# A delta-rule recurrence with an MoE layer on one Trainium2 core: recurrence products on four 64x64 quarters of the array

## The chip, the cores and the metric

The kernel runs on one core of one Trainium2 chip. The metric is device time in microseconds (us), the median of several executions. The core has a TensorE (matrix products, PE in the profile, with its weight loads as PEld), a VectorE (DVE), a ScalarE (ACT), a GpSimd (POOL) and a SyncE (SP), whose queue issues nearly all transfers here. Each engine works through its own list of instructions in order and waits on semaphores for the others.

## The reference

Two parts follow each other. The first is a recurrence over 768 time steps for 4 batches x 8 heads with head size 48:

```
k_n = k / (norm(k) + 1e-06)
for t in range(S):
    y[t]  = q[t] @ state
    v_old = state^T @ k_n[t]
    state = state + beta[t] * outer(k_n[t], v[t] - v_old)
```

The second is an MoE-shaped layer on the 3072 tokens, whose 384 features are all heads' y side by side: `h = x @ w_in` (384 x 2048), an activation `g` that is 0 below -1, h above 1 and (h+1)^2/4 between, and `g @ w_out` (2048 x 384). Everything is fp32.

## The kernel before

The sequence is cut into 12 blocks of 64 steps; block g is worked out for all 32 (batch, head) pairs at once. Two blocks make a group G (0 to 5). Within a block the recurrence is solved in closed form: the Gram matrix of the keys (64x64 for each pair), a triangular solve on it, and four small products by pair, which hang together from block to block through the state SU:

- r (`chain_r`, L338): keys times state, which VectorE subtracts from the values KV (L343);
- u (`chain_u`, L352): the solved triangle XT times r, which ScalarE copies into SU (L356);
- y (`chain_y`, L372): queries times state and masked query Gram times u, the block's output, split by ScalarE and VectorE (L377 to L382) into a rounded part and its rest, for the MoE layer; a fourth of it is moved between partitions by six transfers (xb, L386);
- d (`chain_d`, L396): keys times u, which VectorE adds to the state (L407).

A pair occupies 64 rows of the array: of each two heads one has its keys on rows 0 to 47, the other on rows 64 to 111. A product of r, then, has its stationary operand on one half of the rows and its result on one half of the columns, and the two heads of such a couple lie on opposite halves of both. In u the result stays on the rows' own side. The 32 pairs are 16 such couples (NU), in two halves i of eight (NT, NV); each half has its own tile W (keys, queries, and the masked query Gram that is written back into it), its own KV, its own PSUM bank and its own evictions. `gram` (L146, L147) makes a keys' Gram and a keys-with-queries Gram by one product of 128 moving columns, four couples to a bank.

`lanes`, `solve`, `unlanes` (and their `_whole` forms from group 2 on) solve the triangles of a group's two blocks, largely on VectorE, from the transposition L204 to the transposition into XT (L257, L270); `merge16` and `merge32` finish them with tiny products on 32x32 tiles.

The order is written out by hand. Before the main loop the first group runs alone, with L473 (20 products of 512 columns on idle data) on TensorE while VectorE solves. Weights arrive packed; a generator `unpack` (L125 to L137) unpacks one after the other between other work. In the main loop an item is an up product (L524, 9 instructions), the activation, and a down product two items later (L539). The tables `pe` and `fill` say which small product stands behind which up or down product: `pe` at a whole step comes between up and down, at a half step behind down. `products` issues TensorE's part of all pieces at a step, and `finish` then issues their evictions, those of a half step at the next item's start. In group 0 the items are half as wide at both ends. In a step the last d of a group and the first two Grams of the next stand together. Recurrence products take their PSUM from the two banks `ch`; in the start `spare` hands out all eight.

Loads are issued by SP in the order of the program: xb transfers of a block, W and KV of the block two further on, the stores of finished output.

## Time and profile before

| what | value |
|---|---|
| time, median of 3 runs | 694.93 us (694.51 to 697.15) |
| the profiled execution, first to last instruction (its span) | 693.4 us |
| PE busy | 637.4 us (92%) |
| DVE busy | 437.2 us (63%) |
| ACT busy | 397.7 us (57%) |
| DMA | 41.45 MB, mean 60 GB/s |
| granted clock of TensorE, mean | 0.956 |

The profiled execution has no device time of its own besides the span; the runs' median lies 1.5 us above it. In the page a busy time is the union of an engine's instructions; matmuls are pipelined, so their ends are modelled and a mean duration of one (some 220 ns for a recurrence product) is longer than the pace at which they follow each other. The pace is read from the chain of waits or the timeline: a stage's length divided by its records. An fp32 product leaves two records for each matmul of the program. In the chain of waits each line is the work, or the wait, that the end depended on, with start and length in us.

### The profile page before, as it was taken

How to read it: one execution, taken by the hardware profiler on the slowest of the kernel's cores; microseconds unless marked ns; L12 is line 12 of the kernel's file. 1: busy time of each engine (PE TensorE's matmuls, PEld its weight loads, DVE VectorE, ACT ScalarE, POOL GpSimd, SP SyncE). 2: the span in 40 equal slices, each digit the busy share in tenths (PEclk: the TensorE clock that was granted, in tenths of full speed). 3: DMA queues.
4: the chain of work that ended last, by engine and by line, in shares of the span. 5: the costliest groups of instructions: out<-in, count | busy, mean ns of one | idle time of the engine just before them, and what ended most of it. 6: DMA issues, size and time to landing. Idle time of an engine off the chain costs nothing.

```text
span 693.4 us, 19365 instructions
## 1 busy us (share of the span) xinstructions
PE 637.4 (92%) x8428; PEld 552.6 (80%) x8428; DVE 437.2 (63%) x920; ACT 397.7 (57%) x720; POOL 44.8 (6%) x90
## 2 busy tenths in 40 slices
PE   9848876899999899999999999999999999999996
PEld 7338765678989788888888888788888788889895
DVE  3848788973455896446896447895457894433332
ACT  4227785556656556644457545557555468556663
POOL 3203042001000200000200000200000200000000
PEclk9956896799999999999999999999999999999999
DMA  8960430000161000043100153100242000001001
GB/s 244 418 267 9 120 103 1 0 3 4 24 171 53 24 1 2 18 109 98 46 2 2 41 122 81 28 1 2 60 123 79 9 1 3 14 12 46 0 1 46
DMA packets 18532, 41.45 MB, mean 60 GB/s; under 512 B 3600, under 2 KB 9104, under 8 KB 18448
## 3 DMA queue, kind: packets, MB, share of 16 engines
q1 hardware_dynamic: 18112, 40.04, 20.0%
q8 instruction: 66, 1.08, 0.7%
q14 instruction: 18, 0.15, 0.1%
q0 software_dynamic: 256, 0.08, 0.1%
q10 hardware_dynamic: 80, 0.10, 0.1%
HBM read 33.13 MB, written 4.72 MB: 55 GB/s over the span
## 4 chain that ended last, share of the span: by engine, by line
PE 54%; DVE 29%; ACT 6%; issue 5%; DMA 2%; SPq 2%; POOL 1%; DVEq 0%; POOLq 0%; ACTq 0%
PE o L539 17%; PE h L524 16%; DVE pr L247 5%; DVE A L249 4%; PE ch L146 4%; DVE glo L643 4%; PE ch L372 3%; DVE s L674 3%; PE ch L352 3%; PE ch L324 2%; PE ch L396 2%; DVE A L204 2%; PE ch L308 2%; DMA W<-in_kqa_dram 2%; PE ch L338 2%
## 5 line engine op out<-in xcount | busy, mean ns | idle before, releaser
L524 PE MATMUL h<-xb,wt 128*128 128x512 f32 (+1 forms) x936 | 230.6, 392 | 11.9 <-DVE s L674 10.6
L524 PEld LDWEIGHTS h<-xb,wt 128*128 128x128 f32 x936 | 166.5, 193 | 50.1 <-DVE s L674 15.8
L539 PE MATMUL o<-wt,ghi 128*128 128x384 f32 x768 | 201.7, 344 | 0.0
L539 PEld LDWEIGHTS o<-wt,ghi 128*128 128x128 f32 x768 | 138.9, 190 | 8.6 <-issue 1.5
L674 DVE TENSOR_TENSOR s<-h,s 128x512 f32<-128x512 f32 (+1 forms) x104 | 67.0, 644 | 112.9 <-ACT s L666 112.5
L539 PE MATMUL o<-wt,glo 128*128 128x384 f32 x384 | 130.9, 341 | 5.8 <-DVE glo L643 5.8
L642 ACT CAST ghi<-s 128x512 fp32r<-128x512 f32 (+1 forms) x104 | 61.3, 589 | 110.4 <-DVE s L674 81.4
L647 ACT ACTIVATE s<-h,half 128x512 f32<-128x512 f32 (+1 forms) x104 | 68.0, 654 | 55.8 <-PE h L524 55.1
L643 DVE TENSOR_TENSOR glo<-s,ghi 128x512 fp32r<-128x512 f32 (+1 forms) x104 | 67.1, 645 | 36.3 <-ACT ghi L642 35.9
L539 PEld LDWEIGHTS o<-wt,glo 128*128 128x128 f32 x384 | 72.8, 190 | 8.0 <-DVE glo L643 8.0
L647 ACT ACTIVATE s<-s,one 128x512 f32<-128x512 f32 (+1 forms) x104 | 71.8, 691 | 2.6
L666 ACT ACTIVATE s<-s 128x512 f32<-128x512 f32 (+1 forms) x104 | 62.3, 599 | 3.3
L146 PE MATMUL ch<-W 48*64 48x128 f32 x336 | 43.1, 278 | 9.3 <-ACT W L155 3.7
L146 PEld LDWEIGHTS ch<-W 48*64 48x64 f32 x336 | 37.2, 136 | 14.9 <-issue 5.5
L147 PE MATMUL ch<-W 48*64 48x128 f32 x336 | 43.4, 279 | 0.0
L247 DVE TENSOR_TENSOR pr<-A 128x30 f32<-128x30 f32 (+14 forms) x120 | 39.4, 328 | 5.5 <-POOL A L218 3.3
L249 DVE TENSOR_TENSOR A<-A,pr 128x30 f32<-128x30 f32 (+14 forms) x120 | 39.8, 332 | 4.4
L163 DVE TENSOR_TENSOR W<-ch,mask 64x256 f32<-64x256 f32 x64 | 27.0, 422 | 18.9 <-ACT GG L150 18.1
L150 ACT COPY GG<-ch 128x256 f32<-128x256 f32 x42 | 15.4, 374 | 38.5 <-PE ch L147 38.5
L147 PEld LDWEIGHTS ch<-W 48*64 48x64 f32 x336 | 37.2, 136 | 0.0
L218 POOL TENSOR_SCALAR_AFFINE_SELECT A<-A 128x1024 f32<-128x1024 f32 x4 | 5.1, 1265 | 365.4 <-DVE A L217 365.4
L407 DVE TENSOR_TENSOR SU<-ch,SU 48x384 f32<-48x384 f32 x40 | 22.2, 555 | 9.2 <-PE ch L396 8.5
(137 smaller groups left out, 705.6 us busy)
## 6 DMA issues: line engine op xcount, KB each, us to landing
wt<-in_w_dram SPq DMA_DIRECT2D x16, 768.0 KB, 13.7
KV<-in_kv_dram SPq DMA_DIRECT2D x24, 384.0 KB, 5.7
W<-in_kqb_dram SPq DMA_DIRECT2D x24, 256.0 KB, 4.7
W<-in_kqa_dram SPq DMA_DIRECT2D x24, 192.0 KB, 4.8
out_dram<-wx SPq DMA_DIRECT2D x47, 96.0 KB, 2.2
xb<-X SPq DMA_DIRECT2D x66, 32.0 KB, 2.0
xb<-A SPq DMA_DIRECT2D x6, 32.0 KB, 2.0
beta_sb<-in_beta_dram POOLq DMA_DIRECT2D x8, 10.0 KB, 2.4
```

Source lines behind the costliest of these rows:

```text
L146: nc.tensor.matmul(gp[0:C, p], w_[C:C + D, 0, u, :], w_[C:C + D, 0:2, u, :], start=True, stop=True)
L147: nc.tensor.matmul(gp[C:P, p], w_[0:D, 0, u, :], w_[0:D, 0:3:2, u, :], start=True, stop=True)
L163: nc.vector.tensor_tensor(out=w_[r:r + C, s, us[0]:us[0] + NP], in0=gp[r:r + C, :, 1, :], in1=mask[r:r + C, None, :].broadcast_to([C, NP, ...
L247: nc.vector.tensor_tensor(out=pr, in0=A[:, 0:n, j:j + 1].broadcast_to([P, n, m]), in1=A[:, j:j + 1, j + 1:32].broadcast_to([P, n, m]), op= ...
L249: nc.vector.tensor_tensor(out=A[:, 0:n, j + 1:32], in0=A[:, 0:n, j + 1:32], in1=pr, op=ALU.add)
L524: nc.tensor.matmul(h[:, cols(bs)], WT[f][:, 0, x, k * P:(k + 1) * P], XB[G][:, y, k, cols(bs)], start=(n == 0), stop=(n == 8))
L539: nc.tensor.matmul(oacc[G, k], (ghi, glo)[x][:, k * P:(k + 1) * P], WT[f][:, 1, y, :], start=(new and n == 0), stop=(left[G, b] == 0 and n ...
L642: nc.scalar.copy(out=ghi[:, c], in_=s[:, c])
L643: nc.vector.tensor_tensor(out=glo[:, c], in0=s[:, c], in1=ghi[:, c], op=ALU.subtract)
L647: nc.scalar.activation(out=out, in_=in_, func=AF.Relu, bias=bias, scale=scale)
L666: nc.scalar.activation(out=s[:, c], in_=s[:, c], func=AF.Square)
L674: nc.vector.tensor_tensor(out=s[:, c], in0=h[:, c], in1=s[:, c], op=ALU.max)
```

## The change

Each head's rows get a new place, so that a block's 32 products lie on all four quarters (row half x column half) of the array. A block has one W and one KV tile for both halves of couples (the same bytes, two buffers). H = NU // 2 = 8; the couples are numbered by e (0, 1) and j (0 to 7), and for each j four products follow each other, one to a quarter. `banks` takes two PSUM banks at a time, one for each row half that is read. r, u and d keep 32 products of the same sizes. y keeps 16 products over both halves of the rows (e = 0) and makes the other 16 (e = 1) of two each, an accumulation from both row halves. The Gram is made in two stages, `gram_k` (keys, 32 products of 64 columns) and `gram_q` (keys with queries, 32 of 64 columns), a half step apart; the keys' stage is evicted by two copies of 128x512 in place of four of 128x256, the queries' by four pieces of 64x512 in place of eight of 64x256.

The new places are made by the loads: six for W and ten for KV of a block, where there were four and two. In the start the keys of blocks 0 and 1 are loaded first, by SP and by ACT's queue, then beta, then the queries. Beta's rows are permuted on the chip by a product with a permutation matrix (`perm`, `place_beta`). Ten of the 16 weights are loaded in the start; six (SOON to FT) are issued behind the loads of block 2. What is named `half` in the code before is `mid` now.

```diff
--- before.py
+++ after.py
-    def load_w(g, q=nc.sync):
-        for i in range(NT):
-            x = W[g, i] = sb.tile([P, 3, NV, C], F32, name="W", bufs=4)
-            q.dma_start(out=x[0:C, 0:3:2], in_=kqb[g, i][:, 0:3:2])
-            q.dma_start(out=x[C:C + D, 0:2], in_=kqa[g, i])
-    def load_kv(g, q=nc.sync):
-        for i in range(NT):
-            KV[g, i] = sb.tile([P, 2, NV, D], F32, name="KV", bufs=4)
-            q.dma_start(out=KV[g, i], in_=kv[g, i])
+    def half(x):
+        return slice(x * H, x * H + H)
+    def load_k(g, q, n0=0, n1=1):
+        if g not in W:
+            W[g] = sb.tile([P, 3, NU, C], F32, name="W", bufs=2)
+        x = W[g]
+        lo, hi = slice(2 * n0, 2 * n1 - 1, 2), slice(n0, n1)
+        q[0].dma_start(out=x[0:C, lo, 0:H], in_=kqb[g, 0][:, lo])
+        q[0].dma_start(out=x[C:C + D, hi, 0:H], in_=kqa[g, 0][:, hi])
+        q[1].dma_start(out=x[0:D, lo, H:H + NP], in_=kqa[g, 1][:, hi, 0:NP])
+        q[1].dma_start(out=x[C:C + D, hi, H:H + NP], in_=kqb[g, 1][0:D, hi, 0:NP])
+        q[1].dma_start(out=x[0:D, lo, H + NP:NU], in_=kqb[g, 1][0:D, lo, NP:NV])
+        q[1].dma_start(out=x[C:C + D, hi, H + NP:NU], in_=kqa[g, 1][:, hi, NP:NV])
+    def load_w(g):
+        load_k(g, (nc.sync, nc.sync), 0, 2)
+    def load_kv(g):
+        x = KV[g] = sb.tile([P, 2, NU, D], F32, name="KV", bufs=2)
+        for f in range(2):
+            h, o = slice(f * C, f * C + C), slice(C - f * C, C - f * C + C)
+            nc.sync.dma_start(out=x[C:P, 1, half(f)], in_=kv[g, 0][o, 1])
+            nc.sync.dma_start(out=x[0:C, 1, f * H:f * H + NP], in_=kv[g, 1][h, 1, 0:NP])
+            nc.sync.dma_start(out=x[0:C, 1, f * H + NP:f * H + H], in_=kv[g, 1][o, 1, NP:NV])
+        nc.sync.dma_start(out=x[:, 0, 0:H], in_=kv[g, 0][:, 0])
+        nc.sync.dma_start(out=x[:, 0, H:H + NP], in_=kv[g, 1][:, 0, 0:NP])
+        for f in range(2):
+            nc.sync.dma_start(out=x[f * C:f * C + C, 0, H + NP:NU], in_=kv[g, 1][C - f * C:2 * C - f * C, 0, NP:NV])
...
-    load_w(0)
-    load_w(1)
+    load_k(0, (nc.sync, nc.scalar))
+    load_k(1, (nc.sync, nc.scalar))
     beta_sb = const.tile([P, NS, 32], F32, name="beta_sb")
     nc.sync.dma_start(out=beta_sb[:, 0], in_=beta[:, 0])
+    load_k(0, (nc.sync, nc.sync), 1, 2)
+    load_k(1, (nc.sync, nc.sync), 1, 2)
     weight_loads(0, 2)
     load_kv(0)
     load_kv(1)
-    weight_loads(2, FT)
+    weight_loads(2, SOON)
+    perm = const.tile([P, P], F32, name="perm")
+    nc.gpsimd.memset(perm, 1.0)
+    for c0, base, step, n in ((0, -H, -C, NP), (NP, -C - H - NP, C, NP), (C, -C, C, H)):
+        x = perm[:, 0:C].rearrange("c (a f l) -> c a f l", f=2, l=H)[:, :, :, c0:c0 + NP] if c0 < C else perm[:, C:P].rearrange("c (a f l) -> c a f l", f=2, l=H)
+        nc.gpsimd.affine_select(out=x, in_=x, pattern=[[-16, 4], [step, 2], [-1, n]], base=base,
+                                channel_multiplier=1, compare_op=ALU.is_equal, fill=0.0)
+    def place_beta(n0, n1):
+        b_ps = ps.tile([P, NS, 32], F32, **acc())
+        nc.tensor.matmul(b_ps[:, n0:n1], perm, beta_sb[:, n0:n1], start=True, stop=True)
+        def evict():
+            nc.scalar.copy(out=beta_sb[:, n0:n1], in_=b_ps[:, n0:n1])
+        return evict
     warm = sb.tile([P, P], F32, name="wx")
     nc.vector.memset(warm, 0.0)
...
+    def quarters():
+        return [(e, x) for e in range(2) for x in range(2)]
+    def banks(*shape):
+        return [ps.tile([P, H, *shape], F32, **acc()) for _ in range(2)]
+    def other(e, x):
+        return x if e else 1 - x
+    def gram_k(g):
+        w_, b_ = W[g], banks(C)
+        for j in range(H):
+            for e, f in quarters():
+                k, r, o = w_[f * C:f * C + D, 0, e * H + j, :], f * C, (1 - e) * C
+                nc.tensor.matmul(b_[f][o:o + C, j], k, k, start=True, stop=True)
+        def evict():
+            for f in range(2):
+                nc.scalar.copy(out=GG[:, g % 2, half(f)], in_=b_[f])
+        return evict
+    def gram_q(g):
+        w_, b_ = W[g], banks(C)
+        for j in range(H):
+            for e, f in quarters():
+                r, o = slice(f * C, f * C + D), other(e, f) * C
+                nc.tensor.matmul(b_[f][o:o + C, j], w_[r, 0, e * H + j, :], w_[r, 2 - f, e * H + j, :], start=True, stop=True)
+        def evict():
             def raw():
...
+                for e, f in quarters():
+                    o = other(e, f)
+                    x, y = w_[o * C:o * C + C, 1 + o, half(e)], b_[f][o * C:o * C + C]
+                    nc.scalar.copy(out=x, in_=y)
+                    nc.gpsimd.affine_select(out=x, in_=x, pattern=[[0, H], [1, C]], base=0, channel_multiplier=-1,
                                             compare_op=ALU.is_gt, fill=0.0)
...
             def masks():
...
+                for e, f in quarters():
+                    o = other(e, f)
+                    x, y = w_[o * C:o * C + C, 1 + o, half(e)], b_[f][o * C:o * C + C]
+                    nc.vector.tensor_tensor(out=x, in0=y, in1=mask[o * C:o * C + C, None, :].broadcast_to([C, H, C]), op=ALU.mult)
+            return raw if g < 4 else masks
         return evict
...
+    def chain_r(g):
+        b_ = banks(D)
+        for j in range(H):
+            for e, f in quarters():
+                r, o, k = slice(f * C, f * C + D), (1 - e) * C, e * H + j
+                nc.tensor.matmul(b_[f][o:o + C, j], W[g][r, 0, k, :], SU[r, 1 - f, k, :], start=True, stop=True)
         def evict():
             def after():
...
+                for f in range(2):
+                    v = KV[g][:, 1, half(f)]
+                    nc.vector.tensor_tensor(out=v, in0=v, in1=b_[f], op=ALU.subtract)
             return after
         return evict
+    def chain_u(g):
+        b_ = banks(D)
+        for j in range(H):
+            for e, o in quarters():
+                t, k = 1 - e, other(e, o) * H + j
+                r = slice(t * C, t * C + C)
+                nc.tensor.matmul(b_[t][o * C:o * C + C, j], XT[r, g % 2, k, :], KV[g][r, 1, k, :], start=True, stop=True)
+        def evict():
+            for e, o in quarters():
+                nc.scalar.copy(out=SU[o * C:o * C + C, o, half(e)], in_=b_[1 - e][o * C:o * C + C])
+        return evict
+    def chain_y(g):
+        w_ = W[g]
+        if g % 2 == 0:
+            XB[g // 2] = sb.tile([P, 2, 3, 2 * NB], F32R, name="xb")
+        stg = sb.tile([P, 2, NB], F32R, name="A16" if g == 1 else "X", bufs=1)
+        xb = XB[g // 2]
+        yy = [ps.tile([P, CT, NP, C], F32, **acc()) for _ in range(NT)]
+        def product(i, e, p, o, x, rows, **how):
+            k = e * H + i * NP + p
+            u = (x * NU + k) * D
+            nc.tensor.matmul(yy[i][o * C:o * C + C, e, p], SF[rows, u:u + C], w_[rows, 1 + x, k, :], **how)
+        for i in range(NT):
+            for p in range(NP):
+                for o in range(2):
+                    product(i, 0, p, o, o, (slice(0, C + D), slice(0, P))[o], start=True, stop=True)
+        for p in range(NP):
+            for new in (True, False)[0:1 + (g > 0)]:
+                for i in range(NT):
+                    for o in range(2):
+                        x = o if i == 0 else 1 - o
+                        if new:
+                            product(i, 1, p, o, x, slice(x * C, x * C + C), start=True, stop=g == 0)
+                        else:
+                            product(i, 1, p, o, 1 - x, slice(x * C, x * C + D), start=False, stop=True)
+        def evict():
+            parts = []
+            for i in range(NT):
+                hi, lo = (xb[:, x, :, g % 2 * NB:g % 2 * NB + NB].rearrange("p k (e s t) -> p s e k t", s=CT, t=C)[:, i] for x in range(2))
+                shi, slo = (stg[:, x].rearrange("p (e s t) -> p s e t", s=CT, t=C)[:, i] for x in range(2))
+                nc.scalar.copy(out=hi, in_=yy[i][:, :, 0:3])
+                nc.scalar.copy(out=shi, in_=yy[i][:, :, 3])
+                parts.append((yy[i], hi, lo, shi, slo))
             def after():
...
+                for y, hi, lo, shi, slo in parts:
+                    nc.vector.tensor_tensor(out=lo, in0=y[:, :, 0:3], in1=hi, op=ALU.subtract)
+                    nc.vector.tensor_tensor(out=slo, in0=y[:, :, 3], in1=shi, op=ALU.subtract)
+                for r in (0, C):
+                    for k in range(3):
+                        nc.sync.dma_start(out=xb.bitcast(F32)[r + D:r + C, :, k, g % 2 * NB:g % 2 * NB + NB],
+                                          in_=stg.bitcast(F32)[r + 16 * k:r + 16 * k + 16])
             return after
         return evict
...
+    def chain_d(g):
+        b_ = banks(D)
+        for j in range(H):
+            for e, x in quarters():
+                r, o, k = slice(x * C, x * C + C), other(e, x) * C, e * H + j
+                nc.tensor.matmul(b_[x][o:o + D, j], KV[g][r, 0, k, :], SU[r, x, k, :], start=True, stop=True)
+        def moved():
+            for e, f in quarters():
+                yield SU[f * C:f * C + D, 1 - f, half(e)], b_[other(e, f)][f * C:f * C + D]
         def evict():
             if g == 0:
...
+                for x, y in moved():
+                    nc.scalar.copy(out=x, in_=y)
             def after():
                 if g > 0:
...
+                    for x, y in moved():
+                        nc.vector.tensor_tensor(out=x, in0=y, in1=x, op=ALU.add)
             return after
         return evict
...
@@ -461,11 +537,11 @@
     spare += START
     wu, sv, ln, raws = unpack(), [scale_v(0), scale_v(1)], lanes(0), []
     for g in range(2):
-        for i in range(CB):
-            raws.append(gram(g, i)())
-            if g == 0:
-                raws.pop()()
+        gram_k(g)()
         run(ln, 1)
+    place_beta(0, 1)()
+    for g in range(2):
+        raws.append(gram_q(g)())
     idle = ps.tile([P, 512], F32, **acc())
...
     load_kv(2)
-    for q, r in enumerate(QS):
-        for x in range(2):
-            nc.gpsimd.dma_start(out=beta_sb[r + 16 * x:r + 16 * x + 16, 1:NS, :], in_=beta[q:64:4, 2 + x:ntot:2, :])
+    for x, r in enumerate(QS):
+        for y in range(2):
+            nc.gpsimd.dma_start(out=beta_sb[r + 16 * y:r + 16 * y + 16, 1:NS, :], in_=beta[x:64:4, 2 + y:ntot:2, :])
+    weight_loads(SOON, FT)
     stage(both(chain_r, 1), (wu, 2))
     stage(both(chain_u, 1), (wu, 3))
     spare.clear()
@@ -552,8 +629,8 @@
         where.setdefault(2 * first[G] + int(round(2 * t)), []).extend(x)
     def grams(G, t, g, dt=0.5):
-        for j in range(2):
-            at(pe, G, t + j * dt, *[lambda i=2 * j + x: gram(g, i) for x in range(2)])
+        at(pe, G, t, lambda: gram_k(g))
+        at(pe, G, t + dt, lambda: gram_q(g))
     def plan(G):
...
+            at(pe, G, 1.5, lambda: place_beta(1, NS))
             at(fill, G, 1.5, (load_kv, 3))
             grams(G, 2, a)
             grams(G, 4, b)
```

How instructions moved, at three places. First TensorE, around the last d of group 1 and the first Grams of the next pair of blocks (SU is the state, KV keys and values, ch the two banks, o the output's accumulators). Before:

```order
L524 MATMUL h<-xb,wt_1618 128x512 x9
L396 MATMUL ch<-SU,KV 48x48 x32
L146 MATMUL ch<-W 64x128
L147 MATMUL ch<-W 64x128
...
L539 MATMUL o_4231<-wt_1542,ghi 128x384 x2
```

And now:

```order
L601 MATMUL h<-xb,wt_1777 128x512 x9
L469 MATMUL ch<-SU,KV 48x48 x32
L194 MATMUL ch<-W 64x64 x32
L616 MATMUL o_3266<-wt_1701,ghi 128x384 x2
```

The d products are followed directly by Gram products in both, by 16 of them before (half a block, L146 and L147 in turn), by all 32 of a block's keys now, which begin in both banks.

Second, SP in a group from 1 on: the xb transfers of one block and the loads behind it, up to the next xb. Before:

```order
L386 DMA xb<-X 16x2x256 x6
L72 DMA W<-in_kqb_dram 64x2x512
L73 DMA W<-in_kqa_dram 48x1024
L72 DMA W<-in_kqb_dram 64x2x512
L73 DMA W<-in_kqa_dram 48x1024
L78 DMA KV<-in_kv_dram 128x768 x2
```

And now:

```order
L459 DMA xb<-X 16x2x256 x6
L79 DMA W<-in_kqb_dram 64x2x512
L80 DMA W<-in_kqa_dram 48x2x512
L81 DMA W<-in_kqa_dram 48x2x256
L82 DMA W<-in_kqb_dram 48x2x256
L83 DMA W<-in_kqb_dram 48x2x256
L84 DMA W<-in_kqa_dram 48x2x256
L93 DMA KV<-in_kv_dram 64x384
L94 DMA KV<-in_kv_dram 64x192
L95 DMA KV<-in_kv_dram 64x192
...
L99 DMA KV<-in_kv_dram 64x192 x2
```

Sixteen issues stand between two sets of xb transfers where six stood.

Third, TensorE in the start, up to L473 (L549 now). Before, the whole Gram of block 0 and block 1 stands ahead of it (L146, L147, 64 products). Now:

```order
L137 MATMUL o_143<-wx 128x128 x14
L194 MATMUL ch<-W 64x64 x32
L194 MATMUL h<-W 64x64 x32
L127 MATMUL o_256<-beta_sb,perm 128x32
L207 MATMUL o_259<-W 64x64
L207 MATMUL o_260<-W 64x64
...
L549 MATMUL ch<-SU 128x512 x20
```

The keys' Grams of both blocks come first, then beta's product, then the queries' Grams.

107 lines of the change are left out of this document (20 added, 87 removed).

## The prediction

> **What bounds the kernel now.** I read the shares of the chain that ended last, then the windows by stage, then the chain's pieces in order of time, which carry the sum.
>
> ```profile
> PE 54%; DVE 29%; ACT 6%; issue 5%; DMA 2%; SPq 2%; POOL 1%; DVEq 0%; POOLq 0%; ACTq 0%
> ...
> 75.50:121.00 45.50, 32.93 (x367) 29.76 (x364) 35.84 (x65) 32.27 (x72) 11.03 (x21) 0.84 0.31 81
> ...
> 308.00:410.00 102.00, 98.95 (x1232) 85.61 (x1232) 69.33 (x155) 58.62 (x103) 3.51 (x6) 1.00 0.18 47
> ...
> 613.00:693.00 80.00, 72.94 (x369) 65.65 (x367) 25.67 (x38) 46.39 (x72) 0.00 (x0) 0.98 0.09 23
> ```
>
> TensorE (the first busy time of each window) ends most waits, but not in every stage. A steady group takes 102 us with PE busy for 98.95. From 75.5 to 121 no engine is full: there ACT and DVE hand work to each other. The last 80 us hold no recurrence, so the change cannot touch them. One steady group in the chain (start, length, what):
>
> ```profile
> 281.81 1.14 PE ch L352 x32
> 282.95 2.28 PE o L539 x12
> 285.22 2.02 PE ch L372 x64
> ...
> 289.55 1.57 PE ch L396 x64
> ...
> 293.41 2.00 PE ch L338 x64
> ...
> 323.29 2.31 PE h L524 x9
> ...
> 329.04 1.96 DVE A L204
> ...
> 371.09 1.20 PE ch L308 x63
> ```
>
> From 282.95 (u of the first block done) to 323.29 (last Gram done) PE sets the pace: 40.3 us. From 329.04 to 371.09 the solve on DVE does: 42 us, in which a faster r product (L338) gains nothing. So a PE gain counts in the first stretch only: in groups 1 to 3 whole, in groups 0 and 4 in part.
>
> **The quarters.** A program matmul in fp32 leaves two records, so a stage's 32 matmuls are the x64 above. Do quarters that share rows or columns run at once? These rows bear on it (start, length, records):
>
> ```profile
> 14.22 17.43 PE L473 MATMUL ch<-SU 128*128 128x512 f32 x40
> ...
> 149.74 1.26 PE L281 MATMUL ch<-XT,GG 32*32 32x16 f32 x128 [0.21 <-DVE KV L343]
> ```
>
> A stage of r takes 2.00/64 = 31.3 ns a record, d 24.5, y 31.6. The full array takes 17.43/40 = 436 ns for 512 columns, so 54 ns for 64; y runs at 31.6, hence its two column halves, which share their rows, do overlap. Four 32x32 tiles (L281) take 1.26/128 = 9.8 ns a record against 1.20/64 = 18.8 for two (L308): twice the tiles in half the time, and issue is no bound at 15.6. So I price a stage over four quarters at half: r and u 1.0, with its start 1.05; d 0.8; each Gram (64 records, 64 moving columns) 1.05. The product y keeps 32 records at 31.6 on column halves and adds 64 at 15.6: 1.0 + 1.0, and 0.2 for a second change of shape (L524 takes 2.31 behind a stage, 2.10 with none around it, below): 2.2. But in every row there are as many tiles as column groups. That two row groups run at once in the same columns no row shows. The bounds are 15.6 and 31.3; I take the near end, since L281 and y each show independence along one axis.
>
> The Trainium skill (TensorE: Matmul & The Clock Gate, Part 3, "The mechanism") says that a weight load overlaps a matmul in flight only where the row group differs. By it two quarters on the same rows would take turns and a stage stay near 2.0. y (same rows, 31.6 ns) against r (different rows, 31.3 ns) shows no such penalty.
>
> **The evictions.** A block's products now end in both banks together, so an eviction no longer starts half a stage early. Their prices (busy us, mean ns of one):
>
> ```profile
> L356 ACT COPY SU<-ch 64x384 f32<-64x384 f32 x44 | 20.8, 473 | 5.3 <-PE ch L352 4.6
> L377 ACT CAST xb<-ch 128x384 fp32r<-128x384 f32 x22 | 10.6, 480 | 12.9 <-PE ch L372 12.9
> L378 ACT CAST X<-ch 128x128 fp32r<-128x128 f32 x20 | 5.4, 272 | 0.0
> L328 ACT COPY XT<-ch 32x512 f32<-32x512 f32 x22 | 12.7, 575 | 1.2 <-PE ch L324 0.8
> L150 ACT COPY GG<-ch 128x256 f32<-128x256 f32 x42 | 15.4, 374 | 38.5 <-PE ch L147 38.5
> L155 ACT COPY W<-ch 64x256 f32<-64x256 f32 x20 | 7.4, 369 | 0.3
> ...
> L674 DVE TENSOR_TENSOR s<-h,s 128x512 f32<-128x512 f32 x88 | 60.3, 685 | 102.5 <-ACT s L666 102.4
> L407 DVE TENSOR_TENSOR SU<-ch,SU 48x384 f32<-48x384 f32 x40 | 22.2, 555 | 9.2 <-PE ch L396 8.5
> L381 DVE TENSOR_TENSOR xb<-ch,xb 128x384 fp32r<-128x384 f32 x22 | 12.3, 558 | 15.9 <-ACT X L378 11.2 <-ACT A L378 4.8
> L382 DVE TENSOR_TENSOR X<-ch,X 128x128 fp32r<-128x128 f32 x20 | 5.6, 280 | 0.0
> ```
>
> After u: 4 x 0.473 = 1.9 us, under 2.3 of L539. After y: casts of 0.48 + 0.27, then 2 x (0.558 + 0.280) = 1.7 on DVE: 2.4, where L524 covers 2.3. After d: 4 x 0.555 = 2.2, under L539. But d of the second block is followed at once by the keys' Gram, which starts in both of its banks: 2.25 of naked wait (before, two adds freed the first bank: 1.1, half of it under d's own second half). The queries' Gram leaves four masks of 64x512, priced by L674: 2.75 less 2.3 of cover, 0.45 before the next keys' Gram. Queued behind these waits on PE is the MoE product of that half step.
>
> **The steady stretch**, from u: 2.3, y 2.2, 2.3 + 0.1, d 0.8, 2.3, r 1.05, 2.3, u 1.05 = 14.4; again 2.3, 2.2, 2.4, d 0.8 = 22.1; then 2.25, Gram 1.05, 2.3, 1.05, 2.3, 0.45, 1.05, 2.3, 1.05 = 35.9 us against 40.3: 4.4 less, and 0.2 more in the first u, whose second bank waits for L328 as before.
>
> **SP's queue.** A block's loads become 6 and 10 issues where there were 4 and 2.
>
> ```profile
> 390.79 4.38 SPq L386 DMA_DIRECT2D xb<-X  x6
> 395.26 0.66 SPq L72 DMA_DIRECT2D W<-in_kqb_dram  x1
> 398.03 1.73 SPq L78 DMA_DIRECT2D KV<-in_kv_dram  x2
> ...
> DMA to landing us min/median/max: 4.1/4.8/6.8
> ```
>
> (The last row is that of the kqa loads, L73.) At 0.63 to 0.66 an issue a block takes 3.9 + 6.3 us, and a set of xb copies 3.9. On the clock of the stretch: copies of the first block 6.75 to 10.7, W to 14.6, KV to 20.9, copies of the second from 21.05, when their data are there, W of the second 25.0 to 28.9. Its keys' Gram, at 31.5, needs four of the six loads, begun by 27.0, and half a microsecond later the last two, begun by 28.3: landing after 4.1, which a load of twice the size took, at 31.1 and 32.4. I take 0.4 of wait, bounds 0 and 1.6. Groups 1 to 3: 3 x (4.6 - 0.4 - 0.3, for stages a little above 15.6 ns) = -11.7.
>
> **Group 4** has u, y, d, r, u, y and no Gram: -2.6 by the same terms, +0.3 for y. Behind its last y the copies of xb start 2.4 after the first cast and no more 1.45, as below (610.06 to 611.51): +0.95, together -1.35.
>
> ```profile
> 610.06 0.48 ACT xb L377
> ...
> 611.30 0.21 DVE X L382
> ...
> 640.94 2.10 PE h L524 x9
> ```
>
> **Group 0's tail** has MoE steps of half the size:
>
> ```profile
> 196.55 1.26 PE h L524 x9
> ...
> 192.55 2.49 SPq L547 DMA_DIRECT2D out_dram<-wx  x4
> ...
> 203.59 4.22 DMA W<-in_kqa_dram
> ```
>
> 1.26 does not cover y's 2.4 (1.15 lost, twice) and SP's queue is already last there: with 3.9 + 3.9 + 2.5 (four stores) + 6.3 of issues between the first copies and the second, the fourth load of W begins at 29.3 after u. The same sum as above then gives 36 us to the last Gram, where 34.5 were: +1.3, bounds -1 and +4.
>
> **The start.**
>
> ```profile
> 5.48 6.80 DMA W<-in_kqa_dram
> ...
> 15.62 1.97 DVE A L204
> ...
> 34.42 1.66 PE ch L281 x84
> ...
> 36.42 4.21 issue
> ```
>
> The last W load landed at 12.28. Keys are half the bytes and come by two queues: eight issues of 0.6 on ACT end near 5.6, landing near 8.3, so L204 can start near 11.5 and the first merge near 30.3. But L473's 17.43 us stand on PE behind the queries' Gram, whose 12 loads SP issues until 11.2: landed near 13.3, L473 from 14.5 to 32.0. So the merge gains 2.4, not 4.1; bounds 1 and 2.8. In the first chain stages, behind the merges, ACT's copies and unpacking bind, and only r and u gain: -1.4. The stall of 4.21, one of several between bursts of tiny products, has no releaser; I read it as instructions that come by DMA while weights load. Six of 16 weights leave this stretch: -1.5, bounds 0 and -6. In the first part of group 0, where ACT binds, a block's Gram evictions fall from 4 x 0.374 + 8 x 0.369 = 4.4 to 6 x 0.575 = 3.5, twice, and the last Gram, which ran from 102.80 to 106.2 at a low clock, from 3.4 to near 1.8:
>
> ```profile
> 102.80 0.32 PE ch L146
> ...
> 106.24 0.37 ACT GG L150
> ```
>
> I take -2.5. The six late weights stand on SP ahead of the keys of block 3; ACT's backlog hides that. Without it: up to +3. Placing beta is one product and one copy, under the solve.
>
> **Sum**: -2.4 - 1.4 - 1.5 - 2.5 + 1.3 - 11.7 - 1.35 = -19.6. The profiled execution spans 693.4, 1.5 below the runs' median of 694.93, and I take that 1.5 to lie around the span in both: 675.
>
> **Rivals.**
> - **Column halves bind.** Two row groups in the same columns take turns; it decides from about 25 ns a record on. At 31.3 r and u stay at 2.0, d at 1.6, y takes 3.0, each Gram 2.0. The stretch becomes 35.9 + 1.6 + 1.6 + 1.9 + 3.8 = 44.8, so +4.5 in three groups, +5 in group 0, +3 in group 4, less 4 at the start: 712. For: no row shows otherwise. Against: independence along each axis. A pace half way gives 694.
> - **The banks take the gain.** Every edge above is within 0.3 us of its cover; if each eviction comes 0.5 late, six edges a group cost 3: 675 + 3 x 3 + 2 = 686.
> - **SP takes it.** Loads land 4.8 or more after the issue, and group 0's waits are at their bounds: 3 x 1.2 + 2.7 + 3: 684.
>
> **How the numbers follow.** Forecast (within 6 us of 675) 0.52, banks or SP 0.25, column halves 0.13, a half-way pace 0.06, below 669 with the stalls gone 0.04. The range 661 to 696 takes in the middle cases and the bounds of the start and leaves column halves out; the forecast's own is 669 to 681. About 0.5% (691.5 to 698.4) is what a measurement can tell from no change: faster 0.79, same 0.07, slower 0.14.
>
> **What would show it.** 64 records of r and u near 1.0 us in the steady groups, y near 2.2; from d to the keys' Gram some 2.2 us without PE work; L204 of the first group near 11.5 but the first merge near 32; the 42 us from L204 to the merge unchanged. Stages at 2.0 would make it wrong outright; W loads that end the keys' Gram's wait by over a microsecond in each group would bring 684.

## The result, and the profile after

The changed kernel takes 715.4 us (median of 4 runs, 713.1 to 717.1) where the kernel before took 695.4 beside it: a ratio of 1.0287, 95% interval 1.026 to 1.031. It is slower; the forecast of 675 and its range, 661 to 696, are missed. The profiled execution spans 711.3 us (before 693.4), with a mean granted clock of 0.912 (before 0.956).

From the starts that both profiles show (first up product, the transposition of A, L204 before and L262 after):

| part | before, us | after, us | measured | forecast |
|---|---|---|---|---|
| start, to the first up product | 75.63 | 74.70 | -0.9 | -5.3 |
| front of group 0, to the second transposition | 37.73 | 43.76 | +6.0 | -2.5 |
| rest of group 0 | 113.69 | 123.53 | +9.8 | +1.3 |
| groups 1, 2, 3 | 101.99, 102.02, 102.01 | 103.93, 102.04, 102.97 | +2.9 | -11.7 |
| from the last transposition on | 160.36 | 160.37 | 0.0 | -1.35 |

The steady groups kept their length although the stages became short. Group 2 in the chain of waits of the kernel after (start, length, what):

```profile
398.17 1.16 PE ch L382 x64
399.35 0.57 ACT XT L386
399.93 0.58 ACT XT L386
...
400.56 1.45 PE ch L411 x60
402.01 3.49 PE o L616 x12
405.50 2.17 PE ch L429 x96
...
409.96 0.92 PE ch L469 x62
410.88 2.28 PE o L616 x12
...
413.40 1.14 PE ch L395 x62
...
416.84 1.08 PE ch L411 x64
...
424.65 0.99 PE ch L469 x62
425.64 1.81 issue
...
428.04 1.63 PE ch L194 x62
429.68 3.33 PE o L616 x12
433.01 1.09 PE ch L207 x64
```

The stages are what the forecast wanted: u 1.08, d 0.92 to 0.99, y 2.17, a Gram 1.09 for 64 records (17 ns each). But L616, the same down product that takes 2.28 elsewhere, takes 3.49 behind the first u and 3.33 behind the keys' Gram, and that Gram itself 1.63. Both places stand behind a wait of PE: 1.2 us for the copies of XT (L386), and 1.81 ahead of the keys' Gram. The latter has no releaser in the chain; the timeline of group 1 shows VectorE's four adds of d (L483) there, and PE starting 1.79 after the first of them begins:

```profile
323.32 2.28 DVE L483 TENSOR_TENSOR SU<-ch,SU 48x384 f32<-48x384 f32 x4 [0.55 <-PE ch L469]
...
325.11 0.29 PE L194 MATMUL ch<-W 48*64 48x64 f32 x2 [1.86 <-issue]
325.71 1.68 PE L194 MATMUL ch<-W 48*64 48x64 f32 x62 [0.30 <-issue]
```

What follows the waits is seen in windows, four of group 1 and one of group 4 (window, length, busy time of PE, PEld, DVE, ACT and POOL, granted clock, DMA share, GB/s). They are cut at the edges where the granted clock steps, 3.41 us apart:

```profile
295.40:298.80 3.40, 2.39 (x106) 1.86 (x109) 1.16 (x2) 2.32 (x4) 0.00 (x0) 1.00 0.00 0
298.80:302.20 3.40, 3.40 (x47) 3.31 (x39) 0.00 (x0) 2.50 (x5) 0.00 (x0) 0.50 0.02 5
...
322.70:326.10 3.40, 1.24 (x76) 1.04 (x68) 2.29 (x5) 0.34 (x1) 0.00 (x0) 1.00 0.42 118
326.10:329.50 3.40, 3.40 (x59) 3.28 (x49) 0.00 (x0) 2.06 (x4) 0.00 (x0) 0.50 0.22 49
...
606.00:609.40 3.40, 3.40 (x51) 3.31 (x44) 0.00 (x0) 2.33 (x5) 0.00 (x0) 0.50 0.02 5
```

In the window after the one that holds a wait TensorE gets half its clock: up to 1.7 us, half of 3.41, lost each time. (The last row is the window behind the first u in group 4.) Before, all steady groups ran at 1.00. The stretches between the solves, by windows, after:

```profile
284.00:346.00 62.00, 58.52 (x1181) 50.14 (x1182) 28.71 (x53) 34.40 (x62) 0.00 (x0) 0.92 0.25 63
346.00:388.00 42.00, 38.28 (x252) 33.02 (x252) 38.92 (x95) 23.20 (x37) 3.51 (x6) 1.00 0.07 18
388.00:448.00 60.00, 56.51 (x1181) 48.67 (x1181) 28.61 (x53) 34.29 (x62) 0.00 (x0) 0.94 0.27 66
```

The 42 us of the solve are unchanged, as forecast; the loss is in the stretches at 0.92 to 0.94.

In group 0's tail SP's queue is last. Its timeline (start, length, queue, line, operation):

```profile
199.24 3.25 SPq L624 DMA_DIRECT2D out_dram<-wx  x4
202.58 0.55 SPq L93 DMA_DIRECT2D KV<-in_kv_dram  x1
...
209.07 4.33 SPq L459 DMA_DIRECT2D xb<-X  x6
213.51 0.66 SPq L79 DMA_DIRECT2D W<-in_kqb_dram  x1
...
216.60 0.57 SPq L84 DMA_DIRECT2D W<-in_kqa_dram  x1
```

The fourth load of W for block 5 begins at 215.49, and the keys' Gram of that block comes in parts, each behind loads of W:

```profile
217.74 0.37 PE L194 MATMUL ch<-W 48*64 48x64 f32 x2 [5.00 <-DMA W<-in_kqb_dram]
...
220.63 1.11 PE L194 MATMUL ch<-W 48*64 48x64 f32 x26 [0.15 <-DMA W<-in_kqa_dram]
```

Its last part starts when the sixth load has landed, at 220.6; the first Gram of that block started at 207.95 before. The four pieces behind that part (2.22, 1.92, 2.22 and 1.92 us in the chain) run at half clock. In the start the chain reads:

```profile
13.78 19.93 PE ch L549 x40
33.71 1.37 PE h L339 x96
35.08 5.39 issue
```

(Three more such stops follow, of 3.62, 1.55 and 1.63.) The idle products of the hold (L549) now end last: 19.93 us where the same 40 records took 17.43 before.

In group 0's front TensorE waits for `place_beta`. A window (columns as above) and a line of the timeline:

```profile
83.60:87.70 4.10, 0.27 (x23) 0.14 (x13) 4.04 (x8) 3.14 (x6) 0.00 (x0) 0.94 0.84 254
...
88.35 0.87 PE L127 MATMUL ch<-beta_sb,perm 128*128 128x160 f32 x2 [4.49 <-DVE SU L483]
```

The chain names a weight's transfer there (4.04 us, landed at 87.69), but VectorE does not stand for it: it is busy for 4.04 of the 4.10 us, unpacks weights, works for the MoE layer and reaches the adds of d (L483) only at 86.57. `place_beta` (L127) takes the bank that they read, so it stands 4.49 us on TensorE, and an up product and the first keys' Gram stand behind it. That Gram starts 16.4 us after the first up product (91.1), where the first Gram came after 11.5 before (87.1). From 87.4 to 101 the granted clock is near 0.5; before, it was 1.00 from 80 to 100.

### The profile page after: what moved, and what is told of

Read it like the earlier page. It is cut to its first block, busy times and chain, and to the rows that moved or that the text cites. A ratio compares the mean times of both kernels' runs of the same rounds, so it can differ in the third digit from the quotient of the medians.

```text
span 711.3 us, 21668 instructions
## 1 busy us (share of the span) xinstructions
PE 630.0 (89%) x9552; PEld 540.6 (76%) x9552; DVE 431.4 (61%) x888; ACT 390.2 (55%) x682; POOL 41.4 (6%) x78
## 4 chain that ended last, share of the span: by engine, by line
PE 49%; DVE 28%; SPq 7%; issue 6%; ACT 6%; DMA 3%; POOL 1%; DVEq 0%; ACTq 0%; POOLq 0%
PE o L616 16%; PE h L601 14%; DVE pr L305 4%; DVE A L307 4%; DVE glo L721 4%; DVE s L752 3%; PE ch L549 3%; PE ch L429 2%; PE ch L382 2%; SPq L459 2%; PE ch L194 2%; PE ch L366 2%; DMA W<-in_kqa_dram 2%; PE ch L411 2%; PE ch L207 1%
## 5 line engine op out<-in xcount | busy, mean ns | idle before, releaser
L601 PE MATMUL h<-xb,wt 128*128 128x512 f32 (+1 forms) x936 | 235.5, 399 | 15.5 <-DVE s L752 12.1
L616 PE MATMUL o<-wt,ghi 128*128 128x384 f32 x768 | 211.2, 358 | 0.0
L616 PEld LDWEIGHTS o<-wt,ghi 128*128 128x128 f32 x768 | 146.8, 201 | 7.8
L616 PE MATMUL o<-wt,glo 128*128 128x384 f32 x384 | 135.3, 352 | 6.4 <-DVE glo L721 6.4
L616 PEld LDWEIGHTS o<-wt,glo 128*128 128x128 f32 x384 | 76.5, 199 | 8.5 <-DVE glo L721 8.5
L305 DVE TENSOR_TENSOR pr<-A 128x30 f32<-128x30 f32 (+14 forms) x120 | 39.4, 328 | 5.5 <-POOL A L276 3.3
L194 PE MATMUL ch<-W 48*64 48x64 f32 x704 | 22.0, 258 | 15.5 <-issue 7.7
L194 PEld LDWEIGHTS ch<-W 48*64 48x64 f32 x704 | 18.4, 165 | 19.8 <-issue 15.8
L198 ACT COPY GG<-ch 128x512 f32<-128x512 f32 x22 | 11.8, 589 | 33.6 <-PE ch L194 33.6
L429 PEld LDWEIGHTS ch<-W,SU 48*64 48x64 f32 (+3 forms) x1056 | 24.1, 142 | 4.4 <-ACT SU L415 1.7
L429 PE MATMUL ch<-W,SU 48*64 48x64 f32 (+3 forms) x1056 | 26.7, 230 | 0.6 <-issue 0.5
L455 DVE TENSOR_TENSOR xb<-ch,xb 128x384 fp32r<-128x384 f32 x22 | 12.1, 552 | 24.3 <-ACT X L450 17.8
L222 DVE TENSOR_TENSOR W<-ch,mask 64x512 f32<-64x512 f32 x32 | 21.4, 686 | 7.7 <-PE ch L207 7.4
## 6 DMA issues: line engine op xcount, KB each, us to landing
wt<-in_w_dram SPq DMA_DIRECT2D x16, 768.0 KB, 12.2
```

Source lines behind the costliest of these rows:

```text
L194: nc.tensor.matmul(b_[f][o:o + C, j], k, k, start=True, stop=True)
L222: nc.vector.tensor_tensor(out=x, in0=y, in1=mask[o * C:o * C + C, None, :].broadcast_to([C, H, C]), op=ALU.mult)
L305: nc.vector.tensor_tensor(out=pr, in0=A[:, 0:n, j:j + 1].broadcast_to([P, n, m]), in1=A[:, j:j + 1, j + 1:32].broadcast_to([P, n, m]), op= ...
L429: nc.tensor.matmul(yy[i][o * C:o * C + C, e, p], SF[rows, u:u + C], w_[rows, 1 + x, k, :], **how)
L601: nc.tensor.matmul(h[:, cols(bs)], WT[f][:, 0, x, k * P:(k + 1) * P], XB[G][:, y, k, cols(bs)], start=(n == 0), stop=(n == 8))
L616: nc.tensor.matmul(oacc[G, k], (ghi, glo)[x][:, k * P:(k + 1) * P], WT[f][:, 1, y, :], start=(new and n == 0), stop=(left[G, b] == 0 and n ...
```

## The experiments

Theory: the quarters are worth what they should be, but each stage now ends in both banks at once, so PE waits for whole evictions, and each wait brings a window of half clock; and SP's queue, with 16 issues a block for 6, delays what comes first. Rivals: no gain from quarters; a half clock that comes from the quarters themselves; bytes rather than issues.

**Idle products in the waits.** They take no wait away.

```diff
+    def filler(n):    # into the bank of the next up product
+        for _ in range(n): nc.tensor.matmul(pre[0][:, 0:DM], WT[0][:, 0, 0, 0:P], WT[0][:, 1, 0, :], ...)
+            at(pe, G, T + 11, lambda: filler(5))        # ahead of the first u
+                at(pe, G, T + 14, lambda: filler(12))   # between d and the keys' Gram, G > 0
```

> The changed kernel with idle products (128x384, one pass each, into the bank of the next up product) where PE waits: 12 of them between the last d and the keys' Gram in groups 1 to 3, 5 ahead of the first u in groups 0 to 4. They do no work and take no wait away; they only keep TensorE busy in it. Theory (the wait is what drops the granted clock): the clock is 1.00 in the stretches where it was 0.92 to 0.94, the down product behind the keys' Gram takes 2.3 and not 3.3, each drop avoided gives 1.9: two a group in groups 1 to 3, one in 0 and 4, some -10: 704 to 708. Rival (the clock drops for the quarters' own products or for power): no gain, 714 to 718.

Measured: 712.3 (ratio 1.0242, 1.021 to 1.027), 3 less. In the chain:

```profile
323.62 2.28 PE h L631 x12
325.90 1.32 PE ch L194 x64
327.23 2.12 PE o L616 x11
```

Same wait, filled by the idle products (L631): the down product behind the Gram is back at full pace. So it is the wait that drops the clock, and not the quarters. But the time hardly moved: right behind it the chain stands at W's loads on SP's queue (332.10 4.12 DMA W<-in_kqa_dram). That is the next one.

**Order on SP's queue.** First KV's loads behind the Grams, where they are not yet needed:

```diff
-                at(fill, G, T + 12.5, (load_kv, a + 2))
-                at(fill, G, T + 14.5, (load_kv, b + 2))
+                at(fill, G, T + 16, (load_kv, a + 2))
+                at(fill, G, T + 17, (load_kv, b + 2))
```

> The changed kernel with KV's ten transfers of a block issued later, behind the Grams of the group instead of between xb's copies and the next W (blocks 2 and 3: at the third and fifth step of group 0). Number, size and all else as in the changed kernel. Theory (SP issues in order, and KV's 6.3 us stand ahead of copies and W that are needed first): the keys' Gram of block 5 starts near 214 where it was 220.6, with less low clock behind it, -7; the late weights come 5 us earlier in group 0's front and VectorE's stand of 4.0 us there goes, -4; groups 1 and 3 -1 each: 715 becomes 702 to 706. Rival (the bytes, or the copies' data, set those times): 711 to 715.

Measured: 705.1 (1.013, 1.009 to 1.017), inside the theory's range; the keys' Gram of block 5 begins at 209.0, where it began at 217.7. The front of group 0 became 5.0 us shorter as well, though not for the theory's reason: `place_beta` waits for the adds of d as long as before (4.48 us). Then, in the changed kernel and alone, W's loads half a step earlier:

```diff
-                at(fill, G, T + 12, (load_w, a + 2))
+                at(fill, G, T + 11.5, (load_w, a + 2))
-                at(fill, G, T + 14, (load_w, b + 2))
+                at(fill, G, T + 13.5, (load_w, b + 2))
```

(and block 3's likewise in group 0).

> The changed kernel with W of the block two further on issued half a step earlier, ahead of the six copies of xb, and nothing else (KV stays where it was, between). Theory (order on SP's queue): the keys' Gram of block 5 starts near 214 where it was 220.6, with less low clock, -7; the waits from d to the keys' Gram and for XT stay, since they are evictions, so the steady groups stay at 102 to 103: 705 to 709. Rival (without KV out of the way W gains nothing, since KV's ten transfers of the first block now stand ahead of the copies and of W of the second): 712 to 718.

Measured: 703.8 (1.011, 1.007 to 1.015). In group 0's tail SP now issues W before the copies:

```profile
204.82 0.63 SPq L79 DMA_DIRECT2D W<-in_kqb_dram  x1
...
209.55 4.99 SPq L459 DMA_DIRECT2D xb<-X  x6
```

and the keys' Gram of block 5 starts at 210.46, held only 0.90 us by a mask. The rest of group 0 falls from 123.5 to 114.7, its front from 43.8 to 40.3; the steady groups take 103.6 to 104.1, no less than in the changed kernel, as the evictions' waits stay. Did the order belong to the change? The same edit in the kernel before:

> The kernel before with W of the block two further on issued half a step earlier, ahead of xb's copies (its W are 4 transfers a block). Theory (before, the order did not bind: the Gram that came first waited 1.0 us for W in group 0 only, and nothing in the steady groups): -1 to +1, 693 to 696. Rival (the order would have helped as much): 683 to 688.

Measured: 694.4 beside 695.1 (0.9986, 0.9965 to 1.0007). Before, the order cost nothing.

**The price of the half clock.** The idle products again, now that W is not late:

> The run with W alone moved ahead of the copies (703.8), with the idle products of the filler run in it: 12 between the last d and the keys' Gram in groups 1 to 3, 5 ahead of the first u in groups 0 to 4. Theory (each wait brings a window of 3.4 us at half clock, worth 1.7, and W is no longer the next wait): two a group in groups 1 to 3 and one in group 4 go, -10 to -12: 692 to 694. Rival (the half clock comes out of a wait further on all the same): 699 to 704.

Measured: 694.6 (1.0002, 0.997 to 1.003), 9.2 less than with W's order alone (7.5 by the ratios, give or take 3.5). The stretches between the solves, without idle products and with them:

```profile
272.90:334.40 61.50, 57.98 (x1181) 49.78 (x1181) 28.53 (x52) 34.44 (x62) 0.00 (x0) 0.92 0.28 63
...
480.60:542.10 61.50, 57.98 (x1181) 49.67 (x1182) 28.54 (x52) 34.44 (x62) 0.00 (x0) 0.92 0.27 63
```

```profile
274.20:333.20 59.00, 58.33 (x1198) 49.81 (x1199) 28.59 (x52) 34.41 (x62) 0.00 (x0) 0.97 0.27 66
...
475.90:534.20 58.30, 56.29 (x1198) 48.34 (x1199) 28.59 (x52) 34.29 (x62) 0.00 (x0) 1.00 0.26 67
```

Work that computes nothing shortens a stretch by 2.5 to 3.5 us (3.5 in the middle one, left out here), 9.2 us over the three groups. So some 7 to 9 us of the loss were half clock.

**What the quarters are worth.** Other orders of the same products within a stage: r with the two row halves in turn on the same columns, d with the two column halves in turn on the same rows, the keys' Gram one quarter after the other.

```diff
-        for j in range(H):
-            for e, f in quarters():          # keys' Gram
+        for e, f in quarters():
+            for j in range(H):
```

> The changed kernel with the same products in another order within three stages, to see which quarters run at once: r takes the two row halves in turn on the same columns, d the two column halves in turn on the same rows, the keys' Gram eight products on one quarter after the other. If both kinds of pair run at once: r and d stay near half the array's pace, 2.0 and 1.6 us, and the keys' Gram takes near 4 us (62 ns a record). If a weight load overlaps only products of another row group, as a rule of the Trainium skill (TensorE: Matmul & The Clock Gate, Part 3, The mechanism) says: r 2.0, d 3 or more. If quarters on the same columns take turns: r near 4.

Measured: 733 (one run). Rows of the chain:

```profile
307.03 1.44 PE ch L471 x62
...
310.74 2.04 PE ch L396 x62
...
338.19 3.33 PE ch L194 x64
```

One quarter takes 52 ns a record (the Gram, L194, 64 moving columns), two on the same columns 33 (r, L396, 48), two on the same rows 23 (d, L471, 48), four 15 to 22. The kernel before had its pairs on a diagonal, with neither rows nor columns in common, and r took 31.3 ns there, d 24.5. So either kind of pair keeps about the diagonal's pace: both run at once. The Trainium skill (TensorE: Matmul & The Clock Gate, Part 3, "The mechanism") says that a weight load overlaps products in flight only where the row group differs. By that d on the same rows would be slower than on the diagonal; the measurement says 23 ns, no slower.

The other question, in the best order found below: two quarters at a time in r, u, d and both Grams.

```diff
-        for j in range(H):
-            for e, f in quarters():
+        for e, j, f in [(e, j, x) for e in range(2) for j in range(H) for x in range(2)]:
```

> The best version so far (684.2) with two quarters at a time in place of four: in r, u, d and both Grams the 16 products of one e go first, then those of the other, so that only one pair of quarters is at work. Theory (the quarters' gain is real and shows once the waits are out): from the run of pairs, r +0.85, u +0.9, d +0.5 in each block and 0.9 in each of four Grams, some +8 in a group, less what the earlier eviction of the first half gives back: 684 becomes 705 to 715. Rival (the time is set by loads and evictions, not by the stages): 684 to 690.

Measured: 699.5 (1.0066, 1.004 to 1.009): 15 us slower than with four. r, u, d and a Gram in its chain:

```profile
296.16 2.07 PE ch L395 x62
300.49 1.81 PE ch L411 x64
...
309.03 1.48 PE ch L469 x62
...
312.80 2.08 PE ch L194 x62
```

The stages grew as expected, by 0.5 to 0.9 each, which the expectation put at 21 to 31 us in all; the time lies between theory and rival. A part came back, and the mean granted clock is 0.951 where it is 0.925 with four. I read that as the first half's eviction running under the second, so that PE stands less; no run separates it. Net, the quarters are worth 15 us in this order.

**Weights and the hold.** All 16 weights in the start (SOON = FT):

> The changed kernel with all 16 weights loaded in the start (10 before, 6 behind block 2's loads). Theory: SP's copies of xb, W and KV of block 3 start 3.6 us earlier and VectorE no longer stands 4.0 us for a weight (83.65 to 87.7): -3 to -5 in the front of group 0, little given back in the start: 710 to 713. Rival (the late weights shortened the stalls between the tiny products of the start, and their cover holds): 715 to 717.

Measured: 714.3 (1.0274, 1.024 to 1.031): no difference that can be told. The stops between tiny products grew from 12.2 us to 17.1 (4.77, 4.17, 4.29, 3.82), and of the 4.3 that u of block 0 came later, 2.5 were won back by the second transposition. Each theory has its half, and they cancel. But `place_beta` still waits 4.48 us for the adds of d, with every weight loaded long before: the late weights did not cause that wait. And 15 idle products in the hold (KEEP = 15):

> The changed kernel with 15 idle products in the start in place of 20, nothing else. Theory (the idle products, 19.9 us at a partly low clock, end last ahead of the first merge; the solve is ready near 29.4): the first merge starts near 29.5 instead of 33.7, and some of that reaches group 0: 711 to 713. Rival (the stops between the tiny products absorb it, as they end with the weights' transfers): 714 to 716.

Measured: 710.5 (1.0225, 1.0195 to 1.0255), 4.9 less, better than either expectation. The first merge starts at 31.09 and waits for VectorE's XT. In the profiled execution, the fastest of the four, the start is 2.4 shorter.

**Fewer, larger transfers.** The inputs laid out beforehand in the new places: 4 transfers a block for 16.

```diff
-        q[0].dma_start(out=x[0:C, lo, 0:H], in_=kqb[g, 0][:, lo])      # six like this, ten for KV
+        q[0].dma_start(out=x[0:C, lo], in_=kqb[g][:, n0:n1])
+        q[1].dma_start(out=x[C:C + D, hi], in_=kqa[g][:, hi])
```

> The changed kernel, but its inputs are laid out beforehand in the new places, so that a block's W comes by 2 transfers (64 and 48 rows) and its KV by 2 (values, keys) instead of 6 and 10; the same products, evictions and order, and rows of two tiles in one transfer. Theory (SP's serial issues set the end of group 0's tail and touch group 3): 12 issues of 0.63 us less a block; in group 0's tail the keys' Gram of block 5 starts near 211 where it was 220.6, and the low clock behind that wait shortens, -8 to -10; group 3's end -1; the start -1: 715 becomes 703 to 706. Rival (the landing of the bytes, not the number of issues, sets it): 712 to 716. Rival (the tail waits for the evictions of y and the copies of xb): 709 to 712.

Measured: 716.6 (1.0295, 1.026 to 1.033): no gain. Up to the third transposition it led by 6.2 us (235.7 for 241.9 us); group 2 lost 4.7, the stretch from the last transposition on 4.5, groups 1 and 3 another 1.5. In group 2 PE stops inside y (L418 in that kernel):

```profile
413.22 2.17 PE ch L418 x94
415.39 3.11 issue
418.50 0.27 PE ch L418 x2
```

Two of y's 96 records wait 3.11 us, and nothing that they read is late. Instructions that come by DMA behind large transfers would look like this, but no run isolates it.

**Orders together.** Both keys' Grams first, half a step behind d, alone:

```diff
-                grams(G, T + 14 + (G == 0) / 2, a + 2)
-                grams(G, T + 15 + (G == 0) / 2, b + 2)
+                for j, (f, g) in enumerate(((gram_k, a + 2), (gram_k, b + 2), (gram_q, a + 2), (gram_q, b + 2))):
+                    at(pe, G, T + 14.5 + j / 2, lambda f=f, g=g: f(g))
```

> The changed kernel with the Grams of the next group's blocks in another order: both keys' Grams first, the first of them half a step later than before, so that a down product lies between the last d and it; then both queries' Grams. The last keys' Gram stands where it stood. Theory (evictions at the end of a whole stage leave PE waiting 2.4 us from d to the keys' Gram, and the wait drops the granted clock for some 3.8 us, which costs 1.9 more): in groups 1, 2 and 3 the wait and the low clock behind it vanish, -4 each, and masks no longer stand between the two keys' Grams, -0.4 each; group 0 -1: 715 becomes 700 to 703. Rival (the low clock comes with the Gram's own products, wherever they stand): only the waits go, -2.4 x 3 = 707 to 709.

Measured: 729.0 (1.0458, 1.039 to 1.053), worse: in group 1 the first keys' Gram follows the down product without a wait, but the second needs W of its block, and its last part waits until 336.8. With KV late, merges paired and beta placed later:

```diff
-                        at(pe, G, 10.5 + j + g / 2, lambda f=f, g=g: f(g))   # merge32, groups 1 on
+                        at(pe, G, 10.5 + j, lambda f=f, g=g: f(g))
-            at(pe, G, 1.5, lambda: place_beta(1, NS))
+            at(pe, G, 3, lambda: place_beta(1, NS))
```

> The changed kernel with four edits of order: KV's loads late (as in the run with that alone), both keys' Grams first and half a step behind d, the two blocks' 32-row merges of a kind in one step so that both PSUM banks are free half a step before u, and beta placed a step and a half later. Theory (waits at the ends of whole stages, each with a window of half clock behind it, hide the quarters' gain; the keys' Gram order failed alone only because W of the second block then came too late): over the KV edit alone, -2.7 in each of four groups for u, -3.5 in each of three for the keys' Gram, -3 at beta: 680 to 690. Rival (loads or the instruction stream set the stretch's end whatever the order): 700 to 712.

Measured: 703.9 (1.011, 1.008 to 1.014); the rival held. The first u and the first keys' Gram wait no longer, and the time stands at W instead:

```profile
318.46 5.04 DMA W<-in_kqa_dram
```

With W's loads ahead of the copies in addition:

> The run with the four edits of order (703.9), and in it W of the block two further on issued half a step earlier, ahead of the six copies of xb instead of behind them. Theory (SP stands at the copies until y is cast, 2 us, and issues them for 4.5; W, whose buffer was free when y's products ended, stands behind): in group 1 the second keys' Gram, which waited from 319.6 to 323.5 for W, starts when PE reaches it, its window of half clock goes too, -4 to -5 in groups 1, 2, 3 and in group 0's tail: 686 to 690. Rival (W lands late for the bytes that move then): 699 to 704.

Measured: 692.2 (0.9973, 0.9955 to 0.999), between theory and rival. With three more:

```diff
-            at(fill, G, 0.5, (ln, 1))       # and all of lanes, solve, unlanes, groups 1 on
+            at(fill, G, 0, (ln, 1))         # half a step earlier
-                    at(pe, G, T + 14.5 + j / 2, lambda f=f, g=g: f(g))
+                    at(pe, G, T + 14.5 + j / 2 + (j == 3) / 2, lambda f=f, g=g: f(g))
-KEEP = 20
+KEEP = 15
```

> The same with three more: the four instructions of the lanes and the solve half a step earlier (the keys' Gram is there earlier), the second queries' Gram half a step later (masks of the first block are then done), and 15 idle products on TensorE in the start in place of 20. Theory: VectorE's late XT at the merges (1.7 us in group 1) goes, and the masks' wait (0.4 to 1.9); the first merge, which stood behind the idle products until 33.7, comes at 29.5: -3 a group in three groups and up to -4 at the start over the run before: 674 to 682. Rival (the start's stops between tiny products end with the weights' transfers whenever the merge starts, and the solve's chain fills PE's gain): 684 to 690.

Measured: 684.2 (0.9853, 0.982 to 0.988), the rival's range: 1.5% faster than the kernel before. Of these edits only W's order was tried in the kernel before, where it gained nothing; what the others would give there was not measured. With two quarters at a time the same order gave 699.5 (above), so the order alone does not make the gain in this kernel. Group 1 takes 95.7 us, groups 2 and 3 101.9 and 100.2; in each an up product now waits for the copies that stand behind W:

```profile
303.53 1.98 DMA xb<-X
...
305.59 2.34 PE h L600 x9
```

(L600 is the up product; it waits 1.9 us here, 3.1 and 2.5 in groups 2 and 3.) The same with the copies issued by POOL (`nc.gpsimd.dma_start` in `chain_y`):

> The best version so far (684.2: seven edits of order, six and ten transfers) with the six copies of xb issued by POOL, which is nearly idle, in place of SP. Theory (copies and W stand in each other's way because one queue issues both): the up product that waited 1.9 to 3.1 us for the copies in each group no longer waits, nor drops the clock behind it: -2 to -4 a group in groups 1 to 4: 670 to 677. Rival (POOL takes longer for an issue than SP's 0.63 us, or the copies wait for their data): 681 to 688.

Measured: 685.4 (0.985, 0.980 to 0.990), the rival. With the lanes at their old place:

> As the run with copies issued by POOL, but the lanes and the solve where the changed kernel has them (not half a step earlier). Theory (half a step earlier spares the merges' wait for XT, 1.7 us, at the price of 1.7 more ahead of a down product while VectorE works through the lanes): within 4 us of that run, 670 to 680. Rival (lanes' place decides): 6 or more apart.

Measured: 689.3 (0.991, 0.988 to 0.994), within 4 us of it. The wait for the copies stayed in groups 1 and 2 (3.1 and 1.6 us in the first of the two runs, 2.8 and 1.4 in the second). In group 1 of the first run y's split is done at 302.9 and POOL issues the six copies from 303.5 on, 0.5 us each, but they land 5.5 us after the issue (median), where those of SP took 2.0 at that place: so what is late is the landing, and what it waits for was not separated. The large transfers in the orders of 703.9:

> The same four edits, and the inputs laid out beforehand in the new places (2 transfers for W and 2 for KV of a block). Theory (SP's issues still bind with KV late, 3.9 us of W behind 3.9 of copies): 2 to 6 under the same edits with 6 and 10 transfers, 676 to 686. Rival (large transfers side by side hold up other transfers, as the 3.1 us stop of y at 415 with the DMA at 0.9 in the run with placed loads): no gain or up to 5 over it, 685 to 695.

Measured: 710.8 (1.022, 1.019 to 1.025), 7 more than with small ones, worse than either expectation. And in those of 684.2:

> The same seven edits with the inputs laid out beforehand in the new places (2 transfers for W, 2 for KV). Theory (large transfers bunched ahead of y hold up other transfers, so PE stands in y without a releaser): W ahead of the copies moves the bulk to y's end, so y may stop longer, 1 to 3 us in each group: 2 to 8 slower than the run with 6 and 10 transfers. Rival (the stops came from KV beside W): equal or up to 5 faster.

Measured: 678.5 to 693.7 (0.983, 0.976 to 0.989), not to be told from 684.2.

## Why the prediction was wrong, by its steps

- **The quarters**: right in size, with some luck in the reason. r 1.1 to 1.4 for 1.05, u 1.08, d 0.92 to 0.99 for 0.8, y 2.17 for 2.2, a Gram 1.09 for 1.05. The rival "column halves bind" gave 712, close to the result, and is refuted: pairs on the same columns and on the same rows both overlap. But L281 against L308, one of the two rows that spoke for it, does not show what it was read for: L281 moves 16 columns and L308 32, so the shorter time need not come from the tiles. "The banks take the gain" (686) and "SP takes it" (684) named the right places; neither had the half clock.
- **The evictions**: right in size. From d to the keys' Gram PE waited 1.81 + 0.30 + 0.30 = 2.4 for 2.25; from the merge's end to the first u's it took 2.68, 0.3 more than before, where the sum had 0.2 less; y to d nothing for 0.1. But only their own length was counted.
- **The steady stretch**: this term failed. From the first u's end to the last Gram's end group 2 took 39.4 us (402.01 to 441.4), where 35.9 were forecast and 40.3 stood before. Of the 3.5 missing, half clock took 2.8 (1.2 and 1.05 in the two L616, 0.55 in the Gram). The forecast took the steady groups' clock of 1.00 for granted while making PE stand twice a group, 1.2 and 2.4 us. Another 0.8 went behind the last Gram, where four masks (2.7 us on VectorE) now stand ahead of the transposition. The idle products showed the clock's part: 7 to 9 us over the three groups, of the 14.6 between forecast and measurement.
- **SP's queue**: in the steady groups right as long as PE was slow; it becomes the bound as soon as PE gains (the runs with idle products alone and with the keys' Grams first).
- **Group 0's tail**: wrong in size. From the first u's end (184.0) to the last Gram's (225.9) it took 41.9 us, where 36 were forecast and 34.5 stood before: 7.4 of the 9.8 in that part. The sum over SP's queue came close (the fourth load of W 31.5 after u, for 29.3). It went by that load, while the Gram's last part waited for the sixth. And it left out that PE, having stood 5.0 us up to 217.7, does the four pieces from 220.6 on at half clock (8.3 us). It also took the order of the queue as given: W ahead of the copies alone gave 11.6 back in all, 8.8 of it here.
- **The start**: wrong. The merge came 0.7 earlier, not 2.4: the hold took 19.93 at a partly granted half clock, and was itself last. A shorter hold gave 4.9 in all. The stops came to 12.2 us where they were 11.5 (4.21, 4.17, 1.83, 1.29), not 1.5 less: the six weights fewer saved some 4.9, as the run with all of them shows, and something else in the start cost that again, which stays open.
- **The front of group 0**: wrong, +6.0 for -2.5, and two steps failed. One is "ACT's backlog hides that": W of block 3 is issued 22.5 us after the first up product. With KV late it is issued after 14.6, and 5.0 of the 6.0 came back, although `place_beta` stood as long as before. The other is "Placing beta is one product and one copy, under the solve", a term put at nothing: TensorE stands 4.49 us there. With beta later besides, and the two edits of merges and Grams (the run of 703.9), the stretch took 37.7 us, as before; by these two runs that wait by itself was worth about 1.0.
- **Group 4**: 0.0 for -1.35; the window behind its first u is at half clock too (606.00, above): L616 takes 3.36 there for 2.28 and u 1.59 for 1.08, 1.6 us together, which is more than the 1.35. The copies behind its last y cost 0.96 more, as forecast.

## What to carry to other kernels

Shorter products on the bounding engine pay only as far as the engine does not stand: where a change makes it wait a microsecond or more, price the wait and the half clock that may follow it. When the engine gets faster, look at the order of the transfer queue first: what is needed soonest should not stand behind transfers that wait for their own data. A change that loses as it is may still win in an order of its own: here 1.029 became 0.985. Whether the old kernel would gain from that order too has to be measured before the gain is put down to the change alone.
